# A fused attention and two MLPs on one core: a scratch pool placed over other memory, the last attention spread over fewer groups, and the last sums loaded into other buffers

## The chip, the core and the metric

The kernel runs on one core of a Trainium2 chip. The metric is the device time of one execution in microseconds (us); lower is better. The engines of the core work side by side, each through its own instructions in a fixed order, and wait for each other by semaphores: TensorE (PE in the profile) multiplies matrices into PSUM, VectorE (DVE) and ScalarE (ACT) work element by element and read PSUM, GpSimd (POOL) works element by element in SBUF, and SyncE (SP) issues most of the transfers between SBUF and HBM.

## The reference

Three stages, each in float32, on 2304 tokens (4 batches of 576) of 512 features:

```
def _attn_ref(q, k, v):                       # 4 batches, 8 heads, 576 positions, 64 wide
    scores = scale * q @ k^T + bias, kept where 0 <= i - j < 128
    return softmax(scores) @ v
def _moe_ref(x, w1, w2, w3, w_out):           # 512 -> 768 -> 512
    return np.maximum(np.maximum(x @ w1, x @ w2), x @ w3) @ w_out
def _moe2_ref(x, w_gate, w_val, w_out):       # 512 -> 1536 -> 512
    return silu(x @ w_gate) * (x @ w_val) @ w_out
```

## The kernel before

**Numbers.** Each float32 matrix is split into a rounded head and a rest (`split`, the head by ScalarE at L112, the rest by `low` at L90 on VectorE or GpSimd), and each product is three matmuls (head by head, head by rest, rest by head). The weights arrive as 64-bit words, and `single` makes float32 of them: one pass on ScalarE (L101) and three on VectorE (L104, L105, L107).

**First half: attention and the first MLP.** The tokens of a batch are cut into two parts, so there are eight pairs (batch, part) in `order`. The attention of one pair is twelve units of scores, softmax, transpose and pv. `spread` puts the steps of one list evenly between the groups of another; its argument `early` keeps that many of the last groups free of them. So the attention of pair i+1 lies between the `down_groups` of pair i-1 (second matrix of the first MLP, four output blocks y) and the `up_groups` of pair i (first matrices, 18 groups). Each y block is copied from PSUM to a tile of the pool `tmp` (tag y, L197) and stored to y_dram on ScalarE's queue (L198). TensorE's `ps<-x,w` are the up products, `ps<-h,wo` the down products.

**Second half: the second MLP.** It reads y back (yr, L561) into the pool `raws2` (tag wr2, 5 buffers), forms sums and differences of its blocks (L586, L90) and stores these, split, as ya in a_dram. Each of 12 blocks of the hidden width is a step of seven Strassen-like products over a pair of token blocks; the 12 blocks are taken in three passes of four (`PASS`), and each pass goes over all token pairs. `head`, `tail` and `middle` issue the products of a step (pg and pc in PSUM, L621 to L623) and put them together in a scratch pool `temp`: s1 is ScalarE's copy of the first product (L644), u2 and u3 are sums on VectorE (L630), h0 and h1 hold the silu and the product (L673, L658, L633). TensorE may write to a PSUM bank again only when s1 has been copied from it and u2 added. `down` multiplies by the last matrix (po, L698 to L700), adds the sum of the passes before (acc, loaded from o_dram at L693, pool `accp`, 4 buffers) and stores it (L708).

**The place of the pools.** Pools are taken from both ends of SBUF, in the order in which the code names them. When the first half ends, `mctx.close()` gives back what it held on the right: wraw (raw words of weights), hp (the h tiles), xp (the x tiles) and tmp (the y tiles among them), in the order in which they were taken. The new pools are then laid over that place. With `reuse_waits="tile"` a new tile waits for those old tiles alone whose place it takes.

**What sets the order.** A scheduler orders each engine's instructions when the program is built, from the order of the code, priorities (`tc.high_priority`) and its own estimates of time; on the chip that order is fixed. Stores of ya stay where the code puts them (`keep_in_program_order`).

Of the kernel before, what the change touches and what calls it, by code (L numbers as in the profile page):

```python
# [8 lines left out]
F32 = mybir.dt.float32  # L9
# [11 lines left out]
P = 128  # L21
# [16 lines left out]
SEGMENTS = [(p, c) for p in range(NPASS) for c in (range(PAIRS) if p % 2 == 0 else range(PAIRS - 1, -1, -1))]  # L38
EXTRA = 2
# [1 line left out]

RAWS = 5
C0, C1 = 5, 6
HIGH, EARLY = 100, 3
NORM = "aa"
A2, A3 = 4, 2
WARM, WN = 24, 256
# [10 lines left out]
def kernel(ctx: ExitStack, tc, q0, k0, q1, k1, qk0, qk1, vv, w123, wo1, wgv, wo2, out):  # L58
# [12 lines left out]
    en = lambda *a, **k: ctx.enter_context(pool(*a, **k))  # L71
# [6 lines left out]
    em = lambda *a, **k: mctx.enter_context(pool(*a, side="right", reuse_waits="tile", **k))  # L78
# [10 lines left out]
    def low(eng, out, raw, head):  # L89
        eng.tensor_tensor(out=out, in0=raw, in1=head.bitcast(F32), op=ALU.subtract)  # L90

    def pool_round(out, in_):
        nc.gpsimd.tensor_scalar(out=out, in0=in_, scalar1=1.0, scalar2=1.0, op0=ALU.mult, op1=ALU.mult)
# [30 lines left out]
    def mm3(ps, wt, col, xt_h, xt_l, first, last):  # L124

        wh, wl = wt[:, 0, col:col + P], wt[:, 1, col:col + P]
        nc.tensor.matmul(ps, wh, xt_h, start=first, stop=False)  # L127
        nc.tensor.matmul(ps, wh, xt_l, start=False, stop=False)  # L128
        nc.tensor.matmul(ps, wl, xt_h, start=False, stop=last)  # L129
# [25 lines left out]
    def up_groups(b, s):  # L155

        n = SUBS[s][1]
        m = {}

        def group(f, e):  # L160
            xt = x_t[b, s]
            ps = ps_m.tile([P, 512], F32, tag="m", name="ps1")
            for k in range(KD):
                mm3(ps[:, :n], w1[f, e], k * P, xt[k][:, 0, :n], xt[k][:, 1, :n], k == 0, k == KD - 1)
            with tc.high_priority(HIGH):
                if e == 0:
                    m[f] = tmp.tile([P, 320], F32, tag="m0", name="m0")
                    nc.scalar.copy(m[f][:, :n], ps[:, :n])
                else:
                    nc.vector.tensor_tensor(out=m[f][:, :n], in0=ps[:, :n], in1=m[f][:, :n], op=ALU.max)  # L170
                if e == 2:
                    ht = hp.tile([P, 2, n], F32R, tag=f"h{s}", name=f"h{s}", bufs=NF1)
                    pool_round(ht[:, 0, :], m[f][:, :n])
                    low(nc.gpsimd, ht[:, 1, :], m[f][:, :n], ht[:, 0, :])
                    hs[b, s, f] = ht

        return [lambda f=f, e=e: group(f, e) for f in range(NF1) for e in range(3)]

    def down_groups(b, s):
        t0, n = SUBS[s]  # L180
        t0 += b * S

        def part(ps, d, ks):
            for k in ks:
                ht = hs[b, s, k]
                mm3(ps[:, :n], wo[k], d * P, ht[:, 0, :], ht[:, 1, :], k == 0, k == NF1 - 1)

        def group(ds):

            ps = [ps_m.tile([P, 512], F32, tag="m", name="ps2") for d in ds]  # L190
            for i, d in enumerate(ds):
                part(ps[i], d, range(NF1 - 1))
            for i, d in enumerate(ds):
                part(ps[i], d, [NF1 - 1])
                with tc.high_priority(HIGH):
                    y = tmp.tile([P, 320], F32, tag="y", name="y")
                    nc.scalar.copy(y[:, :n], ps[i][:, :n])  # L197
                nc.scalar.dma_start(out=y_dram[d * P:(d + 1) * P, t0:t0 + n], in_=y[:, :n])  # L198

        return [lambda ds=ds: group(ds) for ds in ((0, 1), (2,), (3,))]  # L200

    order = [(b, s) for b in range(B) for s in range(2)]
# [261 lines left out]
    for t in range(len(units) + LV):  # L464
# [9 lines left out]
        if t < len(units):  # L474
            u = units[t]
            if u.j == BLOCKS[u.s][0]:
                i = todo.index((u.b, u.s, u.p))
# [6 lines left out]
    def attn_units(i):  # L484
        return steps[done_at[i]:done_at[i + 1]]

    def spread(main, *others, early=0):


        done = [0] * len(others)  # L490
        for i, g in enumerate(main):
            for n, o in enumerate(others):
                while done[n] < len(o) and done[n] * (len(main) - early) <= i * len(o):
                    o[done[n]]()
                    done[n] += 1
            g()
        for n, o in enumerate(others):
            for piece in o[done[n]:]:
                piece()


    def second(apool, raws2, ps_o):

        ws, blocks, raw_y, acts, ps, acc, late = {}, {}, {}, {}, {}, {}, {}
# [124 lines left out]
        def add(o, x, y):  # L629
            nc.vector.tensor_tensor(out=o, in0=x, in1=y, op=ALU.add)  # L630
# [53 lines left out]
        def down(g, t, half, pool_=None, tag="o"):  # L684

            p, c = SEGMENTS[g]
            r0 = 2 * c * HT + t * P
            i, tt = divmod(t, HT // P)
            if half == 0:
                ps["o", t] = (pool_ or ps_o).tile([P, 512], F32, tag=tag, name="po", **({} if pool_ else {"bufs": 2}))  # L690
                o = acc[t] = accp.tile([P, 512], F32, tag="acc", name="acc")
                if p:
                    nc.sync.dma_start(out=o, in_=o_dram[r0:r0 + P, :])  # L693
            po = ps["o", t]
            for j in range(2 * half, 2 * half + 2):
                ah, al = [acts[g * PASS + j, i][:, x, tt * P:tt * P + P] for x in range(2)]
                w = ws[p * PASS + j][4]
                nc.tensor.matmul(po, ah, w[:, 0], start=j == 0, stop=False)  # L698
                nc.tensor.matmul(po, ah, w[:, 1], start=False, stop=False)  # L699
                nc.tensor.matmul(po, al, w[:, 0], start=False, stop=j == PASS - 1)  # L700
            if half:
                o = acc.pop(t)
                with tc.high_priority(HIGH):
                    if p:
                        add(o, po, o)
                    else:
                        nc.scalar.copy(o, po)
                nc.sync.dma_start(out=(out if p == NPASS - 1 else o_dram)[r0:r0 + P, :], in_=o)  # L708
# [29 lines left out]
    spread(down_groups(0, 0) + down_groups(0, 1), a2[len(a2) * A2 // 8:] + a3[:len(a3) * A3 // 8])  # L738
    spread(up_groups(*order[2]), a3[len(a3) * A3 // 8:], early=EARLY)
    for i in range(3, len(order) - 1):  # L740
        spread(down_groups(*order[i - 1]) + up_groups(*order[i]), attn_units(i + 1), early=EARLY)
    actx.close()
    raws2 = en("raws2", RAWS, reuse_waits="tile")
    apool = [en("apool", 14, reuse_waits="tile")]
# [6 lines left out]
    spread(down_groups(*order[-1]), conv[21:25])  # L751
    conv = conv[25:]
    mctx.close()
    actp, accp, temp = em("actp", 10), em("accp", 4), em("temp")
    apool.append(en("apool2", EXTRA, reuse_waits="tile"))
    ctx.enter_context(mctx)

    downs, ahead = [], []
    for n, (c, f) in enumerate(STEPS):
        g, j = divmod(n, PASS)  # L760
# [108 lines left out]
```

## Time and profile before

| | |
|---|---|
| time, median of 3 runs | 874.65 us (873.76 to 875.1) |
| time of the profiled execution | 873.95 us |
| its span, from first to last instruction | 872.2 us |
| granted TensorE clock, mean share | 0.992 |
| busy: TensorE, VectorE, ScalarE, GpSimd | 849.7, 593.0, 426.8, 385.3 us |

TensorE is busy nearly all the time, so the other engines' busy times matter only where TensorE waits for one of them. The first half of the kernel ends, and the second begins, at about 441 us of the span.

### The profile page before, as it was taken

The numbers are of one execution on the slowest core, as the hardware profiler recorded it, in microseconds if no ns is written. First come the engines' busy times: TensorE is split into PE (matmuls) and PEld (weight loads), VectorE is DVE, ScalarE is ACT, GpSimd is POOL, SyncE is SP. The second block draws the span as 40 slices with busy tenths as digits, with TensorE's granted clock in tenths as the row PEclk, the third lists the DMA queues.
The fourth block names the chain that finished last, engine by engine and source line by source line (L and its number), as shares of the span: only waits on it lengthen the run. The fifth ranks groups of instructions, "written<-read, shape, count | busy, mean of one in ns | idle before, by whom it ended". The sixth has DMA issues, their size and how long they took to land.

```text
span 872.2 us, 15751 instructions
## 1 busy us (share of the span) xinstructions
PE 849.7 (97%) x5352; PEld 792.9 (91%) x5352; DVE 593.0 (68%) x1551; ACT 426.8 (49%) x1182; POOL 385.3 (44%) x555
## 2 busy tenths in 40 slices
PE   8898999999999999999979899999999999999997
PEld 6687999999999999999969799999999999999996
DVE  7998956767678676657978969995564854434342
ACT  6976747847576565625354545643422422221210
POOL 5575857766877577562522323221421121211110
PEclk9998999999999999999989999999999999999999
DMA  9841514224221330303276586823849322736323
GB/s 328 302 150 56 184 44 138 84 71 128 64 91 56 116 104 19 101 28 121 97 240 254 173 291 239 309 93 104 325 151 311 124 73 72 254 133 222 129 73 120
DMA packets 59088, 130.26 MB, mean 149 GB/s; under 512 B 6272, under 2 KB 17536, under 8 KB 59008
## 3 DMA queue, kind: packets, MB, share of 16 engines
q1 hardware_dynamic: 54400, 124.54, 42.0%
q10 hardware_dynamic: 4608, 4.72, 1.5%
q8 instruction: 42, 0.69, 0.3%
q14 instruction: 38, 0.31, 0.1%
HBM read 93.85 MB, written 35.39 MB: 148 GB/s over the span
## 4 chain that ended last, share of the span: by engine, by line
PE 84%; DVE 6%; DMA 6%; issue 1%; ACT 1%; POOL 1%; SPq 0%; DVEq 0%; ACTq 0%; POOLq 0%
PE ps L127 10%; PE ps L128 10%; PE ps L129 10%; PE pg L621 7%; PE pg L622 7%; PE pg L623 7%; PE po L700 5%; PE po L699 5%; PE po L698 5%; PE pc L621 3%; PE pc L623 3%; PE pc L622 3%; PE pv L405 3%; PE pt L361 2%; PE sc L316 1%
## 5 line engine op out<-in xcount | busy, mean ns | idle before, releaser
L90 POOL TENSOR_TENSOR act<-h,act 128x384 fp32r<-128x384 f32 x72 | 82.6, 1168 | 292.2 <-ACT act L112 260.7
L127 PE MATMUL ps<-x,w 128*128 128x320 f32 (+1 forms) x576 | 173.3, 304 | 0.4 <-ACT w L112 0.3
L129 PE MATMUL ps<-x,w 128*128 128x320 f32 (+1 forms) x576 | 173.6, 302 | 0.1
L128 PE MATMUL ps<-x,w 128*128 128x320 f32 (+1 forms) x576 | 172.8, 301 | 0.0
L621 PE MATMUL pg<-ya,u 128*128 128x384 f32 x360 | 121.9, 339 | 8.4 <-ACT s L644 7.9
L622 PE MATMUL pg<-ya,u 128*128 128x384 f32 x360 | 121.9, 339 | 0.0
L623 PE MATMUL pg<-ya,u 128*128 128x384 f32 x360 | 121.3, 337 | 0.0
L127 PEld LDWEIGHTS ps<-x,w 128*128 128x128 f32 x576 | 109.2, 191 | 3.3 <-ACT w L112 1.1
L129 PEld LDWEIGHTS ps<-x,w 128*128 128x128 f32 x576 | 109.7, 190 | 2.4 <-DVE w L90 1.1
L128 PEld LDWEIGHTS ps<-x,w 128*128 128x128 f32 x576 | 109.7, 190 | 1.3 <-issue 0.9
L377 POOL TENSOR_SCALAR_AFFINE_SELECT t<-pk 128x512 fp32r<-128x512 f32 (+3 forms) x128 | 78.1, 632 | 50.4 <-PE pv L391 15.5
L699 PE MATMUL po<-u,act 128*128 128x512 f32 x216 | 85.2, 394 | 0.0
L700 PE MATMUL po<-u,act 128*128 128x512 f32 x216 | 84.6, 397 | 0.4 <-POOL act L90 0.4
L630 DVE TENSOR_TENSOR u<-pg,s 128x384 f32<-128x384 f32 x72 | 39.7, 554 | 65.9 <-PE pg L623 65.5
L698 PE MATMUL po<-u,act 128*128 128x512 f32 x216 | 84.0, 390 | 0.2 <-ACT act L112 0.2
L621 PEld LDWEIGHTS pg<-ya,u 128*128 128x128 f32 x360 | 68.3, 190 | 13.8 <-ACT s L644 8.6
L329 ACT ACTIVATE z<-z,mn 128x128 f32<-128x128 f32 (+1 forms) x160 | 63.3, 398 | 22.5 <-DVE mn L324 22.0
L622 PEld LDWEIGHTS pg<-ya,u 128*128 128x128 f32 x360 | 68.3, 190 | 4.0
L623 PEld LDWEIGHTS pg<-ya,u 128*128 128x128 f32 x360 | 68.2, 190 | 0.6
L352 ACT ACTIVATE z<-z,rc 128x128 f32<-128x128 f32 (+1 forms) x144 | 49.9, 396 | 22.6 <-DVE rc L343 20.9
L170 DVE TENSOR_TENSOR m<-ps,m 128x256 f32<-128x256 f32 (+1 forms) x96 | 43.1, 450 | 25.8 <-PE ps L129 24.8
L658 ACT ACTIVATE h<-s 128x384 f32<-128x384 f32 x36 | 18.8, 524 | 85.2 <-DVE s L630 85.2
(115 smaller groups left out, 2080.7 us busy)
## 6 DMA issues: line engine op xcount, KB each, us to landing
ya<-a_dram SPq DMA_DIRECT2D x56, 384.0 KB, 4.9
a_dram<-ya SPq DMA_DIRECT2D x42, 384.0 KB, 5.3
wr<-wgv SPq DMA_DIRECT2D x24, 512.0 KB, 5.2
qkr<-qk SPq DMA_DIRECT2D x24, 416.0 KB, 3.5
wr<-w SPq DMA_DIRECT2D x18, 512.0 KB, 5.7
o_dram<-acc SPq DMA_DIRECT2D x36, 256.0 KB, 2.6
acc<-o_dram SPq DMA_DIRECT2D x36, 256.0 KB, 2.7
wr<-wo SPq DMA_DIRECT2D x12, 512.0 KB, 4.4
```

The costliest lines, as they stand in the source:

```text
L90: eng.tensor_tensor(out=out, in0=raw, in1=head.bitcast(F32), op=ALU.subtract)
L127: nc.tensor.matmul(ps, wh, xt_h, start=first, stop=False)
L128: nc.tensor.matmul(ps, wh, xt_l, start=False, stop=False)
L129: nc.tensor.matmul(ps, wl, xt_h, start=False, stop=last)
L329: nc.scalar.activation(out=z[:m, a], in_=z[:m, a], func=AF.Exp, scale=-1.0, bias=mn[:m, a:a + 1], accum_out=sm[:m, a:a + 1],)
L377: nc.gpsimd.affine_select(out=t[:, i, :n, :, :m], in_=w[:, :n, :, :m], compare_op=op, fill=0.0, base=0, pattern=[[0, n], [0, 2], [-sign, m ...
L621: nc.tensor.matmul(o, wh, y[:, 0], start=first and k == 0, stop=False, skip_group_check=True)
L622: nc.tensor.matmul(o, wh, y[:, 1], start=False, stop=False, skip_group_check=True)
L623: nc.tensor.matmul(o, wl, y[:, 0], start=False, stop=k == 1, skip_group_check=True)
L698: nc.tensor.matmul(po, ah, w[:, 0], start=j == 0, stop=False)
L699: nc.tensor.matmul(po, ah, w[:, 1], start=False, stop=False)
L700: nc.tensor.matmul(po, al, w[:, 0], start=False, stop=j == PASS - 1)
```

## The change

Three edits. First, after the first half is closed, `temp` is the first pool to be laid over its place, then `apool2`, which moves from the left end to the right, then `actp` and `accp`; before, `actp` and `accp` came first and `temp` after them. The scratch tiles s1, u2, u3, h0 and h1 then lie over the raw words' pool and the first h tiles, where they lay over x and y tiles. Second, the attention of the last pair in `order` is spread with `early` 9 in place of 3. Third, in the last segment the tiles acc of the last two of six token blocks come from `raws2`.

```diff
-HIGH, EARLY = 100, 3
+HIGH, EARLY, LAST = 100, 3, 9
...
             if half == 0:
...
-                o = acc[t] = accp.tile([P, 512], F32, tag="acc", name="acc")
+                if g == len(SEGMENTS) - 1 and t > 3:
+                    o = acc[t] = raws2.tile([P, 512], F32, tag="wr2", name="acc")
+                else:
+                    o = acc[t] = accp.tile([P, 512], F32, tag="acc", name="acc")
...
     for i in range(3, len(order) - 1):
-        spread(down_groups(*order[i - 1]) + up_groups(*order[i]), attn_units(i + 1), early=EARLY)
+        spread(down_groups(*order[i - 1]) + up_groups(*order[i]), attn_units(i + 1), early=EARLY if i + 2 < len(order) else LAST)
...
     mctx.close()
-    actp, accp, temp = em("actp", 10), em("accp", 4), em("temp")
-    apool.append(en("apool2", EXTRA, reuse_waits="tile"))
+    temp = em("temp")
+    apool.append(em("apool2", EXTRA))
+    actp, accp = em("actp", 10), em("accp", 4)
     ctx.enter_context(mctx)
```

The scheduler then orders some instructions differently. In the rows below a name's number tells tiles of one name apart (the same number in both programs is the same tile here), and the brackets name the semaphores that a row waits for: an engine's, or one of eight DMA semaphores (DMAHW).

ScalarE, at the start of the second half: the copy s1_6994 of the first product of the first step, before. DMAHW5 tells there that a store y_dram<-y has landed.

```order
L101 ACTIVATE wf_7005<-wr_6909 128x512 [waits DMAHW6_49]
...
L197 COPY y_6960<-ps2_6941 128x320 [waits DMAHW0_49,PE_49]
L112 CAST u3_0_6968<-wr_6907 128x512 [waits DVE_49]
L198 DMA y_dram_85<-y_6930 128x320 [waits Activation_49]
L198 DMA y_dram_85<-y_6960 128x320 [waits Activation_49]
L112 CAST u2_3_6830<-wr_6909 128x256 [waits DVE_49]
L101 ACTIVATE wf_7049<-wr_7012 128x512 [waits DMAHW1_49]
L112 CAST u3_1_7019<-tt_7014 128x512 [waits DVE_49]
L112 CAST u3_2_7022<-tt_7014 128x512 [waits DVE_49]
L644 COPY s1_6994<-pg_6987 128x384 [waits DMAHW5_49,PE_49]
```

And with the change (GpSimd's row is the last on the h tile whose place s1_6994 takes):

```order
L197 COPY y_6960<-ps2_6941 128x320 [waits DMAHW0_49,PE_49]
L101 ACTIVATE wf_7005<-wr_6909 128x512 [waits DMAHW7_49]
L644 COPY s1_6994<-pg_6987 128x384 [waits PE_49,Pool_49]
L112 CAST u3_0_6968<-wr_6907 128x512 [waits DVE_49]
L198 DMA y_dram_85<-y_6960 128x320 [waits Activation_49]
L101 ACTIVATE wf_7049<-wr_7012 128x512 [waits DMAHW1_49]
L644 COPY s1_7069<-pg_7062 128x384 [waits PE_49]
```

The copy stands ahead of u3_0, of the last store of y and of the conversions of u2_3, u3_1 and u3_2, and waits for no transfer.

VectorE, at the first sum of the next token pair's blocks (s1_7189, of the loads yr_7104 and yr_7106), before:

```order
L107 SCALAR_TENSOR_TENSOR wr_7012<-wr_7012,wf_7049 128x512 [waits DVE_49,Pool_49]
L630 TENSOR_TENSOR u2_7003<-pg_6996,s1_6994 128x384 [waits PE_49,Activation_49]
L630 TENSOR_TENSOR u2_7078<-pg_7071,s1_7069 128x384 [waits PE_49,Activation_49]
L630 TENSOR_TENSOR u3_7039<-pg_6996,s1_6994 128x384 [waits PE_49]
L630 TENSOR_TENSOR u3_7039<-pc_7041,u3_7039 128x384 [waits DVE_49]
L586 TENSOR_TENSOR s1_7189<-yr_7104,yr_7106 128x768 [waits DMAHW2_49,DMAHW1_49]
L586 TENSOR_TENSOR yr_7104<-yr_7108,yr_7104 128x768 [waits DMAHW3_49,DVE_49,Pool_49]
```

And with the change:

```order
L630 TENSOR_TENSOR u3_7039<-pg_6996,s1_6994 128x384 [waits PE_49]
L90 TENSOR_TENSOR u3_1_7019<-tt_7014,u3_1_7019 128x512 [waits Activation_49]
L531 TENSOR_TENSOR tt_7014<-wr_6907,tt_7014 128x256 [waits DVE_49]
L630 TENSOR_TENSOR u3_7039<-pc_7041,u3_7039 128x384 [waits DVE_49]
L90 TENSOR_TENSOR u3_2_7022<-tt_7014,u3_2_7022 128x512 [waits Activation_49]
L630 TENSOR_TENSOR s1_6994<-pg_6996,s1_6994 128x384 [waits PE_49]
L586 TENSOR_TENSOR s1_7189<-yr_7104,yr_7106 128x768 [waits DMAHW2_49,DMAHW1_49,DVE_49]
L633 TENSOR_TENSOR h1_7087<-u3_7039,h1_7087 128x384 [waits Activation_49]
L586 TENSOR_TENSOR yr_7104<-yr_7108,yr_7104 128x768 [waits DMAHW3_49,DVE_49,Pool_49]
L630 TENSOR_TENSOR u2_7003<-pc_7041,u2_7003 128x384 [waits PE_49]
```

The sums u2 and u3 of the first steps, which stood behind all conversions of the fourth group of weights (u3_0 to u3_4), now stand between them (u2_7003 with pg_6996 is 12 rows ahead of the first row here), and one more sum, s1_6994, stands ahead of s1_7189. On TensorE the order of the products there is nearly the same; pc_7041's first product has moved up into the last groups of the first MLP.

VectorE's last rows, the additions of the last two token blocks, before:

```order
L630 TENSOR_TENSOR acc_10796<-po_10795,acc_10796 128x512 [waits DMAHW5_49,DMAHW4_49,PE_49]
L630 TENSOR_TENSOR acc_10805<-po_10804,acc_10805 128x512 [waits DMAHW7_49,DMAHW6_49,PE_49]
L630 TENSOR_TENSOR acc_10830<-po_10829,acc_10830 128x512 [waits DMAHW0_49,DMAHW4_49,DVE_49,PE_49]
L630 TENSOR_TENSOR acc_10855<-po_10854,acc_10855 128x512 [waits DMAHW5_49,DMAHW1_49,DVE_49]
L865 UNCONDITIONAL_BRANCH
```

And with the change:

```order
L630 TENSOR_TENSOR acc_10796<-po_10795,acc_10796 128x512 [waits DMAHW7_49,DMAHW6_49,PE_49]
L630 TENSOR_TENSOR acc_10805<-po_10804,acc_10805 128x512 [waits DMAHW1_49,DMAHW0_49,PE_49]
L630 TENSOR_TENSOR acc_10855<-po_10854,acc_10855 128x512 [waits PE_49]
L630 TENSOR_TENSOR acc_10830<-po_10829,acc_10830 128x512 [waits PE_49]
L869 UNCONDITIONAL_BRANCH
```

The two additions have changed places, and neither waits for a transfer of its own; their two loads stand some 70 rows further up in SyncE's order, between loads of acc and stores to o_dram of the segment before. TensorE finishes po_10854 before po_10829 in both programs.

## Rows read from the trace of the kernel before

**Rows 1.** Page: busy time (share, instructions), granted clock in 40 slices, tenths

```profile
PE 849.7 (97%) x5352; PEld 792.9 (91%) x5352; DVE 593.0 (68%) x1551; ACT 426.8 (49%) x1182; POOL 385.3 (44%) x555
...
PEclk9998999999999999999989999999999999999999
```

**Rows 2.** Windows: length, busy PE, PEld, DVE, ACT, POOL (instructions), clock, DMA share, GB/s

```profile
450.00:454.00 4.00, 0.00 (x0) 0.00 (x0) 4.00 (x10) 1.94 (x4) 0.00 (x0) 0.81 1.03 406
454.00:458.00 4.00, 3.21 (x10) 3.21 (x11) 1.72 (x4) 3.21 (x5) 1.30 (x1) 0.50 0.98 299
...
494.00:498.00 4.00, 2.55 (x13) 2.23 (x14) 4.00 (x9) 1.22 (x3) 0.00 (x0) 1.00 0.69 181
```

**Rows 3.** Chain of waits around the second half's start: start, length, what

```profile
446.49 7.69 DMA y_dram<-y
454.26 0.49 ACT s L644
...
490.07 2.70 DMA yr<-y_dram
```

**Rows 4.** Timeline of TensorE: start, length, what, [idle before, released by]

```profile
446.40 0.34 PE L622 MATMUL pg<-ya,u 128*128 128x384 f32 x1
...
448.13 0.34 PE L623 MATMUL pg<-ya,u 128*128 128x384 f32 x1
454.79 0.69 PE L621 MATMUL pg<-ya,u 128*128 128x384 f32 x1 [6.32 <-ACT s L644]
...
459.37 0.34 PE L623 MATMUL pg<-ya,u 128*128 128x384 f32 x1
```

**Rows 5.** Window, as in rows 2, of the second half's first 57 us

```profile
442.89:500.00 57.11, 48.04 (x249) 44.90 (x249) 50.80 (x88) 29.61 (x59) 16.23 (x11) 0.94 0.64 226
```

**Rows 6.** Timeline of VectorE

```profile
447.27 1.68 DVE L105 SCALAR_TENSOR_TENSOR wf<-wr,wf 128x512 int32<-128x512 int32 x1
448.98 0.69 DVE L107 SCALAR_TENSOR_TENSOR wr<-wr,wf 128x512 int32<-128x512 int32 x1
...
454.77 1.02 DVE L630 TENSOR_TENSOR u<-pg,s 128x384 f32<-128x384 f32 x2
460.26 0.56 DVE L630 TENSOR_TENSOR u<-pg,s 128x384 f32<-128x384 f32 x1 [4.47 <-PE pg L623]
...
461.33 0.95 DVE L586 TENSOR_TENSOR s<-yr 128x768 f32<-128x768 f32 x1
...
476.34 0.42 DVE L104 TENSOR_SCALAR wf<-wf 128x512 int32<-128x512 int32 x1
```

**Rows 7.** Timeline of SyncE's queue: the second load of y

```profile
451.82 1.15 SPq L561 DMA_DIRECT2D yr<-y_dram  x1
```

**Rows 8.** DMA issues in 451.9 to 452.5 us: count, size, us from issue to landing

```profile
yr<-y_dram SPq DMA_DIRECT2D x1, 384.0 KB, 8.2
```

**Rows 9.** Window, as in rows 2, within the last attention

```profile
360.00:400.00 40.00, 40.00 (x333) 39.60 (x332) 22.55 (x70) 14.54 (x47) 20.99 (x41) 1.00 0.17 58
```

**Rows 10.** Timeline of TensorE after the last pv

```profile
394.29 0.56 PE L405 MATMUL pv<-t,v 128*128 128x128 f32 x4
...
399.17 0.28 PE L128 MATMUL ps<-h,wo 128*128 128x256 f32 x1
399.29 0.28 PE L129 MATMUL ps<-h,wo 128*128 128x256 f32 x1
...
400.74 0.31 PE L127 MATMUL ps<-x,w 128*128 128x320 f32 x1
```

**Rows 11.** Timeline of GpSimd: the last x tile

```profile
396.43 0.32 POOL L90 TENSOR_TENSOR x<-xr,x 128x64 fp32r<-128x64 f32 x1
```

**Rows 12.** Timeline of VectorE, its last two additions

```profile
867.97 1.29 DVE L630 TENSOR_TENSOR acc<-po,acc 128x512 f32<-128x512 f32 x2 [3.58 <-DMA acc<-o_dram]
```

**Rows 13.** Chain of waits, near its end

```profile
864.80 3.05 DMA acc<-o_dram
```

**Rows 14.** Timeline of TensorE, its last matmul

```profile
867.37 0.39 PE L700 MATMUL po<-u,act 128*128 128x512 f32 x1
```

## The prediction

> **What bounds the kernel now.** I read the page first, then the busy time in windows, then the chain of waits, and last the timelines of the engines that the chain names. The page says that TensorE is busy for 849.7 of 872.2 us, and that its granted clock is below the top level in two places only, at the start and in the slice around 450 us [rows 1]. So a gain has to come out of the few microseconds in which TensorE stands, and a loss can come from any wait that is added anywhere else. The windows find the largest stand: from 450 to 454 us TensorE does nothing, and from 454 to 458 it works at a granted clock of 0.50, which is 1.2 GHz [rows 2]. VectorE is busy all through the first of these windows. The chain of waits names the reason: TensorE's matmul at 454.79 waits for ScalarE's copy of s, and that copy waits for a transfer of y to y_dram that was issued at 446.49 and landed 7.69 us later [rows 3]. That copy needs nothing from the transfer; its output tile only lies on the place of the y tile that is being read.
>
> The timeline of TensorE gives the price: from 446.40 to 448.13 it starts ten matmuls, 0.173 us apart; then it stands for 6.32 us, and the fifteenth matmul after that of 448.13 starts at 459.37 [rows 4]. That is 11.24 us for what 15 x 0.173 = 2.60 us would do. **TensorE alone thus lost 8.6 us here**, 6.5 of it by standing and 2.1 by the low clock, and that is the most that edit 1 can give.
>
> But VectorE runs closer to its own limit than the page's 68% suggests. Between 442.89 us (the moment at which it starts on the words of the fourth group of weights) and 500 us it is busy for 50.80 of 57.11 us, so 6.31 us are idle [rows 5], of which 4.47 us are one piece, before 460.26, where it waits for the TensorE matmuls that came late [rows 6]. In 494 to 498 us it is TensorE that waits (2.55 of 4 us busy, at a granted clock of 1.00) while VectorE is busy for all 4 [rows 2]. The work of VectorE in this stretch is the same in both programs, so what TensorE gains beyond VectorE's idle time it gives back before 500 us.
>
> **Edit 1, the scratch's place.** In the new order ScalarE's copy s1_6994 waits for TensorE and for a GpSimd operation on the words whose place it takes, and no transfer, and stands ahead of the four conversions it used to follow. The second matmul group of pg_6987 then finds its bank copied, and TensorE passes 448.13 without stopping. What is late next is VectorE. I add up its rows in the new order from 447.27 on, with the durations of the old trace [rows 6]: the sum u2_7003 is put in ahead (0.5 us, half of the 1.02 that two took), and the L105 operation that took 1.68 us there ends by 449.5. Up to the sum s1_7189 there follow six conversions of 512 words (0.69 long, 0.6 apart: 3.6 us), six short ones (0.35 apart: 2.1) and four sums (2.0); with 0.3 us for the words of wr_7012 that is 457.5 us. There s1_7189 needs two y loads. The second of them was issued at 451.82 [rows 7] and took 8.2 us [rows 8], so it landed at 460.0; I keep that time, because the transfers ahead of it are the same in number and size, and the queues' share is 1.03 in the window before [rows 2]. So VectorE waits 2.5 us. Behind that wait stand h1_7087 and the sum u2_7003 with pc_7041, for which TensorE's pc_7209 waits in turn.
>
> The result for VectorE: 460.0 in place of 461.33 at s1_7189 [rows 6], with one more sum (0.5 us) behind it, so 1.8 us ahead. The rest of its old idle time, 6.31 - 4.47 = 1.8 us, was spent on a TensorE that was late and now is early; I take it as gained. **Edit 1: -3.6 us, taken as -3.5**, with 1.8 and 6.3 us as the bounds (the later idle time comes back; no wait for the loads at all). As a check, the new order does five more of VectorE's sums and differences before the L104 operation that the old trace has at 476.34 [rows 6], and by the same adding up reaches it at 474.5 us: 1.8 + 2.4 = 4.2 us ahead, inside the bounds.
>
> A place of uncertainty is TensorE's clock: while VectorE waits for the loads, TensorE stands for some 3 us before pc_7209. The rows show one stand of 6.32 us after which the clock was low, and a window with 1.45 us of waiting in which it stayed at 1.00 [rows 2, 4]; 3 us lies between. If the clock falls as before, TensorE loses up to 2.1 us, which costs nothing as long as VectorE is what it waits for. The Trainium skill (TensorE: Matmul & The Clock Gate, Part 1) says that the low clock is the default state and that activity releases it; this speaks against the change, which trades one long stand for several shorter ones, and by it the lost clock would come again. Were it then not hidden, the gain of edit 1 would be 1.4 us and not 3.5.
>
> **Edit 2, the last attention over fewer groups.** Its 12 units now go between 21 groups of order[5] and order[6], with 9 in place of 3 kept free. The work is the same; TensorE has 40.00 of 40 us busy in 360 to 400 and VectorE 22.55 [rows 9], so nothing can be won, and each wait would count in full. The place where it bites first is the last x tile: the last pv ends at 394.85, GpSimd finishes x 1.9 us later, at 396.75 [rows 11], and the matmuls that need it start at 400.74 [rows 10]. In the new order 33 matmuls lie between, and the shorter of their two kinds starts every 0.12 us [rows 10]: at least 4.0 us, against the 1.9 that the chain takes. So it holds, with 2.1 us to spare. **Cost 0.** Without that cover it costs what the chain is late, 1:1.
>
> **Edit 3, the last sums.** VectorE's two last additions begin at 867.97 and take 1.29 us together, having waited for the loads issued at 864.80, which took 3.05 us [rows 12, 13]; TensorE ends at 867.37 + 0.39 = 867.76 [rows 14]. The loads now stand much earlier in SP's order, and the sum whose matmuls end first stands first. One addition is left after TensorE, from about 867.9: the end moves by 0.65 + 0.07, **-0.7 us**. The two loads stand between loads of the same kind on SP, and wait for VectorE operations close to those that their neighbours wait for; at worst they hold SP's queue for one VectorE operation, under 1 us, where TensorE's rows have no gap.
>
> **The sum** is -3.5 + 0 - 0.7 = -4.2 us. The profiled execution took 873.95 us, 0.70 below the median of the runs (874.65), so 869.75 for such an execution and **870.4 us for the median**.
>
> **The rivals.**
> *VectorE does not bind.* If the loads land earlier than I assume, or the work that is late on VectorE is not what TensorE needs, all of 8.6 us comes back: 874.65 - 8.6 - 0.7 = 865.35. For it: the 1.45 us that TensorE waits in 494 to 498 could be filled by work that is ready. Against it: VectorE's 4.00 of 4 us in that window [rows 2].
> *The wait moves.* The loads of y take the place of the store of y: VectorE's wait is longer than 2.5 us, or the low clock comes back and is not hidden. With 1.8 us won and 2.1 lost edit 1 gives nothing, and the tail's 0.7 us is all: 873.95, no difference to be seen. For it: the transfers take 0.98 to 1.03 of the engines' time in 450 to 458 [rows 2], and a chain link of 2.70 us on the yr loads is already there at 490 [rows 3].
> *Slower: the last attention in too few groups.* Scores, softmax and pv of a unit have less time between them, and TensorE waits in order for a pv that is not ready. Each of the 12 units would then cost its wait; at 0.6 us a unit that is 7 us, so 874.65 - 4.2 + 7.2 = 877.65. It decides against the change from 0.35 us a unit (4.2 in all). For it: TensorE has no gap there that could take it up; against it: VectorE is idle for 17 of 40 us [rows 9].
>
> **How the numbers follow.** The forecast has 0.66 and its own range goes from 867.6 (6.3 + 0.7 us gained) to 872.2 (1.8 + 0.7). Full recovery has 0.12, the moved wait 0.14, and the slower case 0.08. The range from 865.3 to 873.4 takes in full recovery and the edge of the moved wait, and leaves out the rest of that and the slower case. A change of under 0.2% (1.75 us) can't be told from none in this kernel: faster means below 872.9, slower above 876.4. Faster gets 0.66 + 0.12 + 0.02 of the moved wait, same the other 0.12 and 0.01 of the slower case, slower 0.07.
>
> **What would show it.** In the new trace TensorE should have no stand over 2 us between 446 and 456, and ScalarE's first L644 copy should lie near 446. A wait of VectorE for DMA yr of about 2.5 us before 460 shows edit 1's limit; none there, with TensorE waiting less than 1 us in all up to 500, shows the first rival. TensorE should keep 40.00 of 40 us in 360 to 400 us. After the last matmul one addition of some 0.65 us should be left. The forecast is wrong if VectorE is busy for under 52 us of the same 57, or if TensorE has gaps among the pv matmuls.

## The result, and the profile after

The changed kernel takes 862.99 us (median of 4 runs, 862.85 to 863.15) against 874.2 us of the kernel before beside it: a ratio of 0.9871, 95% interval 0.9854 to 0.9888. It is 11.2 us faster; 4.2 us were forecast, and the time lies below the range. The profiled execution's span is 861.4 us, 10.8 us shorter.

The page's lines on busy time and on the granted clock, as in [rows 1]:

```profile
PE 847.5 (98%) x5352; PEld 791.9 (92%) x5352; DVE 588.4 (68%) x1551; ACT 426.0 (49%) x1182; POOL 382.2 (44%) x555
...
PEclk9998999999999999999999999999999999999999
```

The second dip of the clock is gone. The windows over the start of the second half, in the kernel before (columns as in [rows 2]):

```profile
440.00:480.00 40.00, 33.58 (x180) 32.68 (x179) 30.92 (x49) 19.82 (x38) 11.28 (x8) 0.91 0.72 262
480.00:520.00 40.00, 37.34 (x191) 33.27 (x190) 34.24 (x63) 20.36 (x42) 12.13 (x9) 1.00 0.67 231
500.00:520.00 20.00, 20.00 (x103) 18.16 (x102) 14.36 (x24) 9.87 (x20) 7.18 (x7) 1.00 0.83 306
442.89:521.71 78.82, 69.75 (x359) 64.71 (x359) 65.89 (x113) 40.01 (x80) 23.41 (x17) 0.96 0.69 247
```

and after:

```profile
440.00:480.00 40.00, 38.07 (x204) 36.27 (x203) 35.08 (x64) 24.25 (x48) 12.93 (x9) 0.96 0.83 281
480.00:520.00 40.00, 40.00 (x212) 37.33 (x211) 35.79 (x64) 22.29 (x47) 12.55 (x11) 1.00 0.74 261
500.00:520.00 20.00, 20.00 (x107) 18.71 (x106) 15.83 (x28) 10.86 (x23) 6.39 (x6) 1.00 0.71 254
444.91:512.54 67.63, 65.92 (x346) 62.31 (x347) 63.15 (x112) 38.75 (x80) 22.07 (x16) 0.97 0.80 286
```

**Where the time came from.** From 440 to 520 us TensorE stood for 6.42 + 2.66 = 9.1 us before and stands for 1.9 us now. The low clock after its stands cost it 4.58 - 14 x 0.173 = 2.2 us before (the 14 steps from 454.79 to 459.37 [rows 4]) and costs it 3.36 - 10 x 0.173 = 1.6 us now (the 10 steps from 447.78 to 451.14, below). Together that is 7.7 us. The mean clock of the windows would give more, but before the change a part of its 0.91 fell into the stand itself (0.81 from 450 to 454 us, with TensorE at 0.00 [rows 2]), where no work was lost. The end after the last matmul gives 0.9 us (below). The other 2.2 us of the span are not placed by such rows; some 1.5 us of them lie in this stretch, since u2_7564 (below) starts 9.2 us earlier than before. The same program in two executions (edit 1 alone, in two of the experiments) had spans of 863.1 and 861.7 us.

The last row of each block is VectorE from one and the same instruction to another (its first on the fourth group's words, the sum u2_7564 with pc_7640). It does the same 112 instructions between them. Before that took 78.82 us with 12.93 us idle; after, 67.63 us with 4.48 us idle and 2.74 us less for the instructions themselves.

TensorE, ScalarE and VectorE of the changed kernel at the place of [rows 4], in timelines:

```profile
445.81 0.45 PE L621 MATMUL pg<-ya,u 128*128 128x384 f32 x1 [1.12 <-ACT y L197]
447.78 0.69 PE L621 MATMUL pg<-ya,u 128*128 128x384 f32 x1 [0.65 <-ACT y L197]
...
451.14 0.34 PE L622 MATMUL pg<-ya,u 128*128 128x384 f32 x1
...
461.18 0.44 PE L621 MATMUL pc<-ya,u 128*128 128x384 f32 x1 [0.16 <-DVE u L630]
```

```profile
447.30 0.42 ACT L197 COPY y<-ps 128x320 f32<-128x320 f32 x1 [0.98 <-DMA y_dram<-y]
...
448.19 0.47 ACT L644 COPY s<-pg 128x384 f32<-128x384 f32 x1
```

```profile
449.15 0.54 DVE L630 TENSOR_TENSOR u<-pg,s 128x384 f32<-128x384 f32 x1
...
457.91 0.54 DVE L630 TENSOR_TENSOR s<-pg,s 128x384 f32<-128x384 f32 x1
458.38 0.94 DVE L586 TENSOR_TENSOR s<-yr 128x768 f32<-128x768 f32 x1
```

The copy of s waits for no transfer, and no stand of TensorE is over 1.2 us. The two longer ones end with ScalarE's copies of y, one of which still waited 0.98 us for a store of y. VectorE goes from s1_6994 to s1_7189 without a wait: the second load of y, issued at 452.26, took 3.9 us and landed at 456.2, not at 460.0:

```profile
452.26 0.37 SPq L561 DMA_DIRECT2D yr<-y_dram  x1
```

```profile
yr<-y_dram SPq DMA_DIRECT2D x1, 384.0 KB, 3.9
```

The end, to be read beside [rows 12, 14]: one addition after the last matmul, which ends at 857.84.

```profile
857.88 0.69 DVE L630 TENSOR_TENSOR acc<-po,acc 128x512 f32<-128x512 f32 x1 [2.03 <-PE po L703]
```

```profile
857.45 0.39 PE L703 MATMUL po<-u,act 128*128 128x512 f32 x1
```

### The profile page after: what moved, and what is told of

Same layout as the page of the kernel before. It is cut to its first block, busy times and chain, and to the rows that moved or that the text cites. A ratio compares the mean times of both kernels' runs of the same rounds, so it can differ in the third digit from the quotient of the medians.

```text
span 861.4 us, 15755 instructions
## 1 busy us (share of the span) xinstructions
PE 847.5 (98%) x5352; PEld 791.9 (92%) x5352; DVE 588.4 (68%) x1551; ACT 426.0 (49%) x1182; POOL 382.2 (44%) x555
## 4 chain that ended last, share of the span: by engine, by line
PE 87%; DVE 5%; DMA 4%; ACT 1%; issue 1%; POOL 1%; SPq 0%; DVEq 0%; ACTq 0%; POOLq 0%
PE ps L128 10%; PE ps L127 10%; PE ps L129 10%; PE pg L622 7%; PE pg L623 7%; PE pg L621 7%; PE po L703 6%; PE po L702 6%; PE po L701 6%; PE pc L621 3%; PE pc L622 3%; PE pc L623 3%; PE pv L405 3%; PE pt L361 2%; PE sc L316 1%
## 5 line engine op out<-in xcount | busy, mean ns | idle before, releaser
L101 ACT ACTIVATE wf<-wr 128x512 f32<-128x512 f32 (+1 forms) x66 | 41.5, 632 | 37.6 <-DMA wr<-wgv 20.9
```

## The experiments

Each ratio is to the kernel before, run beside it on the same chip, with its 95% interval; 0.001 is 0.87 us.

### Edit 1 alone, edit 2 alone, edit 3 alone, and the last two together

```diff
 # edit 1 alone
-    actp, accp, temp = em("actp", 10), em("accp", 4), em("temp")
-    apool.append(en("apool2", EXTRA, reuse_waits="tile"))
+    temp = em("temp")
+    apool.append(em("apool2", EXTRA))
+    actp, accp = em("actp", 10), em("accp", 4)
```

> Edit 1 alone: the scratch's place, with the last attention and the last sums as before. Theory A (the store of y that ScalarE's first copy of s waits for is nearly the whole cause, and VectorE's sums may run ahead of its conversions once it is gone): 10 us faster, near 864.3, TensorE standing less than 2.5 us in 440 to 520, the second load of y landing before 458, two additions of 1.3 us left after the last matmul. Theory B (edit 1 only gives TensorE's stand back, up to 8.6 us, and edit 2's new order gives the rest): 6 to 8.6 us faster, 866 to 868, with waits of TensorE left in 486 to 502. The theory of the prediction (VectorE binds): 3.5 us faster, near 870.7.

> Edit 2 alone: the last attention spread with 9 groups kept free, the scratch as before. Theory A: no difference over 1 us (873.2 to 875.2), the stand of some 6 us before TensorE's pg matmul still there. Theory B: 1.5 to 2.5 us faster, since the new order of the last attention lets the second half's first loads and sums run earlier. The slower rival of the prediction: 3 us slower or more, with gaps among the pv matmuls.

> Edit 3 alone: the last two sums' tiles from the raw buffers. Both theories: 0.7 us faster (873.5), one addition of 0.65 us after the last matmul, everything up to 860 us as before. If the early loads hold SyncE's queue: no gain or a loss, with waits between 640 and 720 us.

> Edits 2 and 3 without edit 1. Theory A: 0.7 us faster (873.5), the sum of the two alone, and the long stand kept; 10.5 us slower than the whole change. Theory B: 2.2 to 3.2 us faster.

| kernel | ratio | interval | us |
|---|---|---|---|
| edit 1 alone | 0.9895 | 0.9882 to 0.9909 | -9.2 |
| edit 2 alone | 0.9994 | 0.9983 to 1.0005 | -0.5 |
| edit 3 alone | 0.9987 | 0.9978 to 0.9995 | -1.1 |
| edits 2 and 3 | 0.9989 | 0.9979 to 0.9998 | -1.0 |

Edit 1 is nearly the whole gain, and it alone gives more than twice what the prediction allowed it. Its 9.2 us (interval 7.9 to 10.3) lie between theory A's 10 and theory B's 8.6. For A speak the 2.0 us in all that TensorE stands from 440 to 520, and edit 2, which gives 0.5 us and not B's 1.5 to 2.5; but the second load of y landed at 458.1 us, a little after what A had named. With edit 2 alone the long stand stays; the row is from TensorE's timeline of that kernel:

```profile
453.98 0.69 PE L621 MATMUL pg<-ya,u 128*128 128x384 f32 x1 [5.69 <-ACT s L644]
```

With edit 3 alone the end has the one addition that was forecast (VectorE's timeline of that kernel; its last matmul ends at 867.72):

```profile
867.76 0.69 DVE L630 TENSOR_TENSOR acc<-po,acc 128x512 f32<-128x512 f32 x1 [2.03 <-PE po L703]
```

In the kernel with edit 1 alone the load of y does land late enough to hold VectorE, for 1.49 us, and TensorE keeps three stands of under 0.8 us in 440 to 480, all of them before that wait ends (timelines of that kernel; in the second profile of the same program, further down, the first of the three is 2.19 us long):

```profile
458.19 0.96 DVE L586 TENSOR_TENSOR s<-yr 128x768 f32<-128x768 f32 x1 [1.49 <-DMA yr<-y_dram]
```

```profile
449.60 0.44 PE L621 MATMUL pg<-ya,u 128*128 128x384 f32 x1 [0.73 <-DVE u L630]
453.10 0.44 PE L621 MATMUL pg<-ya,u 128*128 128x384 f32 x1 [0.48 <-ACT h L673]
454.80 0.44 PE L621 MATMUL pg<-ya,u 128*128 128x384 f32 x1 [0.37 <-DVE u L630]
```

So a wait of VectorE for that load, which the prediction counted in full, is there, and TensorE's timeline lists no stand after it up to 480 us.

### The whole again, and the whole without edit 2

The second kernel is edits 1 and 3, with `early=EARLY` for every attention.

> The whole change again, on the same chip as the three below. 10 to 11.5 us faster than before (0.987 to 0.9885).

> Edits 1 and 3 without edit 2. If edit 2 is worth nothing by itself: within 0.8 us of the whole change. If its order of the last attention gives the whole change what edit 1 alone lacks (9.2 us against 11.2): 1.3 us or more slower than the whole change.

0.9868 (0.9851 to 0.9885) and 0.9879 (0.9861 to 0.9896). The medians are 1.1 us apart, between what was expected if edit 2 is worth nothing and if it is worth something; the intervals overlap, and what edit 2 is worth beside edit 1 these runs can't tell.

### The store's wait taken off, the order kept

```diff
-    actp, accp, temp = em("actp", 10), em("accp", 4), em("temp")
-    apool.append(en("apool2", EXTRA, reuse_waits="tile"))
+    apool.append(em("apool2", EXTRA))
+    actp, accp, temp = em("actp", 10), em("accp", 4), em("temp")
```

> Only the second pool of ya tiles moves to the right end, ahead of the others; the scratch stays last. ScalarE's first copy of s then waits for no store of y, but it stands behind the conversions as in the kernel before, and VectorE's rows have the order of before, with u2_7003 behind all conversions (it waits for stores of y in place of the copy). If the wait of the copy is the cost, whatever the order: 6 us faster or more. If the place in the order is what counts (the copy and the sums ahead of the conversions): 0.5 to 2 us faster, with a stand of TensorE of 4 us or more left.

0.9977 (0.9965 to 0.999), 2.0 us faster. The copy of s waits for no store any more, but stands where it stood, and so do VectorE's sums. (The sum u2_7003 now waits for stores in its place, and VectorE's timeline shows no idle time that a store ended.) TensorE's, ScalarE's and VectorE's timelines of this kernel, and its window as in [rows 2]:

```profile
451.75 0.69 PE L621 MATMUL pg<-ya,u 128*128 128x384 f32 x1 [3.79 <-ACT s L644]
```

```profile
451.22 0.85 ACT L644 COPY s<-pg 128x384 f32<-128x384 f32 x2
```

```profile
457.47 0.56 DVE L630 TENSOR_TENSOR u<-pg,s 128x384 f32<-128x384 f32 x1 [3.10 <-PE pg L623]
```

```profile
480.00:520.00 40.00, 37.37 (x192) 33.41 (x191) 33.21 (x62) 18.95 (x40) 12.65 (x9) 1.00 0.69 242
```

The stand is 3.79 us, a little under the 4 us expected, and TensorE's waits in 480 to 520 us are all still there (2.63 us against 2.66). ScalarE's timeline of the kernel before agrees: the last conversion ahead of the copy ended at 452.94, and only after it did ScalarE stand for the store, for 1.32 us.

```profile
454.26 0.86 ACT L644 COPY s<-pg 128x384 f32<-128x384 f32 x2 [1.32 <-DMA y_dram<-y]
```

Of edit 1's 9 us only some 2 come from the wait for the store as such. By subtraction the rest comes from the order, in which the copy and the sums stand ahead of the conversions; that order with the wait left in was not tried.

### More work for VectorE

On top of edit 1 the sum s1_7189 is done five times, then nine times (s1_7189's result is the same each time).

```diff
-        made, keep = [0], []
+        made, keep, again = [0], [], []
...
-            nc.vector.tensor_tensor(out=o, in0=raw_y[x], in1=raw_y[y], ...)
+            for _ in range(5 if name == "S1" and len(again) == 1 else 1):
+                nc.vector.tensor_tensor(out=o, in0=raw_y[x], in1=raw_y[y], ...)
+            again.append(0) if name == "S1" else None
```

> Edit 1 alone, and four more sums of 0.95 us each on VectorE (the sum s1_7189 is done five times, into the same tile, with the same result), 3.8 us in all at 458 to 470. If VectorE binds TensorE up to 500 us, as the prediction had it: 3 to 4 us slower than edit 1 alone, 867 to 868.5. If VectorE's idle time after 500 us takes work up and TensorE needs only the sums that stand ahead: 0 to 1.5 us slower than edit 1 alone, 864 to 865.8.

> Edit 1 alone once more, beside the two below: 8 to 10 us faster than before.

> Edit 1 alone with eight more sums of 0.95 us on VectorE in place of four (7.6 us in all, the same tile and result). If VectorE binds up to 500 us: 7 us slower than edit 1 alone. If it has some 4 to 5 us of idle time left there before TensorE has to wait (edit 1's trace shows 4.8 us idle for VectorE between 441.7 and 512.8): 1.5 to 4 us slower than edit 1 alone, and TensorE waits for s or u of VectorE between 465 and 520.

| kernel | ratio | interval |
|---|---|---|
| edit 1 and 3.8 us for VectorE | 0.9902 | 0.9883 to 0.9921 |
| edit 1 alone, again | 0.9899 | 0.988 to 0.9917 |
| edit 1 and 7.6 us for VectorE | 0.9972 | 0.996 to 0.9984 |

The first 3.8 us cost 0.3 to 0.6 us, within the intervals nothing. The second 3.8 us cost about 6 us (0.007); the two together cost more than the 1.5 to 4 us that I expected if VectorE has some room, and nearly the 7 us expected if it has none. So VectorE has room for about 4 us here; with 7.6 us more it does bind. In the last kernel TensorE waits for the next tokens' tiles ya, which ScalarE and VectorE make after the added sums (TensorE's timeline of that kernel):

```profile
475.28 0.62 PE L623 MATMUL pg<-ya,u 128*128 128x384 f32 x2 [0.71 <-ACT ya L112]
480.02 0.44 PE L624 MATMUL pc<-ya,u 128*128 128x384 f32 x1 [1.81 <-DVE ya L90]
```

The low clock is a part of why this came to 6 us and not to 4. Windows as in [rows 2], of the last kernel and of edit 1 alone beside it:

```profile
442.00:520.00 78.00, 71.16 (x362) 64.16 (x361) 71.80 (x123) 40.25 (x83) 26.29 (x17) 0.98 0.70 252
442.00:520.00 78.00, 74.38 (x390) 68.20 (x389) 71.80 (x124) 42.96 (x91) 22.79 (x19) 1.00 0.74 261
```

TensorE stood for 3.2 us more, and after the wait of 1.81 us the clock was low for a while, some 0.02 x 78 = 1.6 us. That is 4.8 of the 6.4 us between the spans of these two executions (868.1 and 861.7 us); the rest is open.

### The loads of y later

Edit 1, and four stores more on SyncE's queue ahead of the loads:

```diff
         def load_y(c):
+            if c == 1:
+                for x in range(4):
+                    tc.keep_in_program_order(nc.sync.dma_start(out=d_dram[x]..., in_=blocks[0, "A11"][0]...))
```

> Edit 1 alone with four more stores of a ya tile (384 KB each, to a place that nothing reads) on SyncE's queue ahead of the four loads of y, so that these land some 4 us later, the second near 462. The order of VectorE's rows is then another one at this place: the first sums of the next tokens stand behind six more of the sums that TensorE waits for. If the loads' landing sets the end of the stretch (the prediction's 460 us): 3 us slower than edit 1 alone or more. If only VectorE's sums for TensorE have to be early, and the next tokens have time: within 1.2 us of edit 1 alone.

0.99 (0.9882 to 0.9919), the same as edit 1 alone. VectorE's timeline:

```profile
462.59 0.96 DVE L592 TENSOR_TENSOR s<-yr 128x768 f32<-128x768 f32 x1 [1.87 <-DMA yr<-y_dram]
```

The sum that needs the load starts at 462.59, against 458.19 and 456.30 in the two executions of edit 1 alone; VectorE waits for the load, and the time is the same. Part of that is that six more sums stand ahead of the wait in this order; a late load with the old order behind it wasn't tried.

## Why the prediction was wrong

**The step that failed** is the one under what bounds the kernel: "The work of VectorE in this stretch is the same in both programs, so what TensorE gains beyond VectorE's idle time it gives back before 500 us." From it came VectorE as the bound of edit 1, and its 3.5 us in place of the 8.6 us of TensorE's own loss. Edit 1 alone gave 9.2 us. Two things were wrong in the step; a third one stands below because it looks like a reason and is none.

*A busy VectorE was taken for one that TensorE waits for.* VectorE's rows up to 500 us also hold work with time to spare: conversions of weights and tiles of the next tokens. 3.8 us more of such work cost nothing that could be measured. In the window of 4.00 of 4 us busy in [rows 2] TensorE's longest wait was not for VectorE: it was for ScalarE's copy of s, which stood behind two conversions for the next tokens (TensorE's and ScalarE's timelines, before).

```profile
495.30 0.45 PE L621 MATMUL pg<-ya,u 128*128 128x384 f32 x1 [1.63 <-ACT s L644]
```

```profile
493.39 0.93 ACT L112 CAST ya<-yr 128x384 fp32r<-128x384 f32 x2 [1.45 <-issue]
...
494.77 0.48 ACT L644 COPY s<-pg 128x384 f32<-128x384 f32 x1
```

So the needed copy stood behind work that could come later, and VectorE's being busy beside it did not show that VectorE was short of time. (What held those conversions for 1.45 us the trace does not name.) With edit 1's order the waits in 480 to 520 went from 2.66 us to 0.3 and 0.2 us, and to none in the changed kernel; with the old order kept they stayed.

*The stretch was cut at 500 us.* VectorE has 5.64 us idle from 500 to 520 in the kernel before (its window above), which I did not count. From its first instruction here to u2_7564 it was idle for 12.93 us, not 6.31 us [rows 5]; 8.45 of these are gone (8.2 and 7.7 in the two profiles of edit 1 alone).

*The durations were taken as fixed*, and this did not matter. In [rows 6] an operation that takes 0.69 us elsewhere took 1.68 while GpSimd worked beside it. With the change GpSimd's first conversion runs while VectorE waits for words (until 444.91), in GpSimd's timeline:

```profile
441.56 1.31 POOL L90 TENSOR_TENSOR u<-wr,u 128x512 fp32r<-128x512 f32 x1 [5.33 <-ACT u L112]
```

and the same 112 instructions of VectorE take 2.74 us less. That GpSimd is the reason is read from which instructions were shorter, and wasn't tried by itself. But this came with edit 2. VectorE between the same two instructions, as in the windows of the result, in the two profiles of edit 1 alone and in that of edit 2 alone:

```profile
441.69:512.84 71.15, 69.17 (x369) 64.34 (x368) 66.39 (x113) 38.68 (x79) 22.41 (x17) 1.00 0.75 272
439.77:511.56 71.79, 68.17 (x359) 62.52 (x358) 66.55 (x113) 38.50 (x79) 22.44 (x17) 1.00 0.76 269
444.17:520.21 76.04, 66.67 (x342) 61.25 (x342) 63.80 (x113) 39.50 (x79) 21.85 (x16) 0.96 0.71 253
```

Edit 1 alone gives its 9.2 us with VectorE as busy as before (65.89 us), and edit 2 alone has the shorter instructions and gives 0.5 us.

The sign that the prediction named for its being wrong, VectorE busy for under 52 of the 57 us, did not come: from 444.91 to 502.02 it was busy for 54.8 us. A busy VectorE fitted both accounts.

**Edit 1, the parts.** Right: the copy without the store, and the long stand gone. Left open there was the clock: a shorter drop is left in the changed kernel (0.96 in place of 0.91 in 440 to 480), and none in the two profiles of edit 1 alone (1.00). Wrong: the load's landing, 456.2 for 460.0. SyncE began its row of stores 2.4 us earlier (443.27 against 445.63). Its size mattered little, as the late loads show. The check by adding up VectorE's rows gave 4.2 us; it ended at 474.5 us and had the same fault. The prediction took the store's 7.69 us [rows 3] for the reason of the stand; ScalarE stood for it for 1.32 us only, and the conversions ahead of the copy were the larger part. That the order is worth more than the wait the prediction did not see; the kernel with the order kept shows it.

**Edit 2** at nothing: right within what the runs can tell (-0.5 us alone, interval -1.5 to 0.4). TensorE has 40.00 of 40 us busy in 320 to 360 and in 360 to 400 in the changed kernel, as was said, so the slower rival did not come. **Edit 3**: -0.7 us forecast, 1.1 measured (0.4 to 1.9), and the one addition left; the early loads held up nothing that shows.

**The rivals.** The first, that VectorE does not bind (865.35 us, 0.12), was nearest in its mechanism and still 2.4 us short; it gave back the one long stand and none of the shorter waits in 486 to 502 us, and 0.45 us of the 2.4 come from the kernel before, which took 874.2 us beside the result and 874.65 us in the prediction. Its sign came in part: VectorE had no wait for the loads, but TensorE still waited 1.9 us. The second rival's time did not come; VectorE's longest wait for these loads was 1.87 us, in the kernel with the late loads. Of the clock's loss 1.6 of 2.2 us came again in the profiled execution. The sentence from the Trainium skill (TensorE: Matmul & The Clock Gate, Part 1), by which the change would bring the low clock back, is half borne out: after stands of 1.12 and 0.65 us, eight matmuls took 0.52 us in one execution, and in another execution of the same program, after stands of 0.83 and 0.58, none did.

## What to carry to other kernels

An engine that is 100% busy beside a waiting one binds only if the row that is waited for is its own, or follows from one of its own, and nothing stands ahead of that row that could come later; read which engine ends the wait, ask of each row by when it is needed, and look for idle time past the end of the stretch before calling an engine full. Where a scheduler orders the work, a false dependence can cost more than its wait, since rows are ordered late because of it: here 2 us for the wait and some 7 for the order. A scratch buffer is better not laid over a buffer that a late store still reads; over raw words and h tiles it cost nothing that shows here.

## What the runs showed that I had not expected

The low clock after short stands is not a fixed thing of the program. The changed kernel in its first profile lost about 1.6 us to it in 440 to 480 us (0.96), and in the second none:

```profile
440.00:480.00 40.00, 37.52 (x205) 34.90 (x204) 35.69 (x65) 24.20 (x48) 13.31 (x9) 1.00 0.83 283
```

There TensorE stood longer (2.48 us against 1.93), and the span was 861.9 against 861.4 us. In the second profile of edit 1 alone the clock stayed at 1.00 even after a stand of 2.19 us (TensorE's timeline of that kernel):

```profile
447.70 0.45 PE L621 MATMUL pg<-ya,u 128*128 128x384 f32 x1 [2.19 <-DVE u L630]
```

And VectorE's work got cheaper by 2.74 us over 68 us without one instruction less, which changed the time by nothing that can be told.
